# A transformer block on one core: the order of the first loads, and copies of two transposed tiles in pieces

## The chip, the cores and the metric

The kernel runs on one core of a Trainium2 chip. The metric is the time on the device in microseconds (us) of one execution; lower is better. A core has a matrix engine (TensorE, PE in the profile), three engines for elementwise work (VectorE or DVE, ScalarE or ACT, GpSimd or POOL), a queue for transfers and barriers (SyncE or SP) and 16 DMA engines that all queues share. The engines run side by side and wait for each other by semaphores.

## The reference

```python
def _A_ref(x, wqkv, w_phi, wo):          # H = 32 heads of Dh = 20, D = 640
    qkv = (x @ wqkv) ...                  # q, k, v by head
    pq = einsum("bhsd,hdf->bhsf", q, w_phi); pk = einsum("bhsd,hdf->bhsf", k, w_phi)
    phi_q = concatenate([softmax(pq), softmax(-pq)]); phi_k = concatenate([softmax(pk), softmax(-pk)])
    kv = einsum("bhsf,bhsd->bhfd", phi_k, v); z = phi_k summed over s
    o = (phi_q @ kv) / (phi_q . z + 1e-6)
    return o @ wo
def _B_ref(x, w_gate, w_up, w_down):      # F = 1536
    return (gelu(x @ w_gate) * (x @ w_up)) @ w_down

h  = x + _A_ref(layernorm(x), ...)        # x: 1 x 2048 x 640, bfloat16
h2 = h + _B_ref(layernorm(h), ...)
```

A block with linear attention over a feature map and a gated feed-forward part; both read a layer norm of their input.

## The kernel before, in words

The 2048 rows of x are 16 tiles of 128 rows (tile t), in four blocks of four (`x_sb[0]` holds tiles 0 to 3). The 640 columns are five chunks of 128. A tile is normalised, transposed into `LN1T` (chunk by chunk, so that the contraction lies on the partitions), and then multiplied with W_v, with W_k folded with w_phi (`Wk2`), and later with W_q folded with w_phi. After that come the attention's output and the feed-forward part. The queues of all engines hold their instructions in the order in which the code writes them; the order in the head of the kernel is written out by hand.

The change lies in the head, the first 12 us:

- **Transfers.** SP issues x tile 0 (L189), x tile 1 (L190), x tile 2 (L193), W_v chunks 0 and 1 (L194), chunks 2 and 3 (L195), x tile 3 (L196), W_v chunk 4 (L197), x tiles 4 and 5 (L198), and then five transposing loads of W_k into `WkT` (L203). ACT's queue issues w_phi (L191) and then loads the table of ACT's functions (L192). w_phi has one reader, DVE's `BD` (L433), which `fold` needs.
- **TensorE's filler.** `warm` runs matmuls on a constant, with no use for their result, at the start (L230) and after the first transposes (L447).
- **Tiles 0 and 1.** DVE takes the mean off (`ln_0`, `xc_a`), TensorE transposes the five chunks into a PSUM tile (`tr_c`, by `transpose_to`, L164), and ACT copies the whole into `LN1T` (L165). The scale of the norm is applied when v is evicted (`v_ev`, L316).
- **Tile 2 and tile 3.** `ln_st` takes two half statistics (L121) and their aggregate (L125) on DVE, ACT makes the inverse root out of a logarithm and an exponential (L131, L132; `log` says when they are queued), DVE normalises (`ln_ap`, L156), TensorE transposes, and DVE copies (`ln_tp`, L165). `between` queues something between the two half statistics: for tile 3 it is the transposing and copying of tile 2.
- **v.** `v_part(t, chunks)` multiplies the named chunks of tile t with those of W_v, two matmuls of 320 columns a chunk, into one PSUM tile (L312). PSUM has four such buffers here, taken in turn by filler, transposes and accumulators.
- **What comes next.** After v of tile 2 (`v_part(2, ...)`) TensorE transposes tile 3 and folds W_k (L248), and the loop over the tiles begins.

Of the kernel before, what the change touches and what calls it, by code (L numbers as in the profile page):

```python
# [8 lines left out]
BF16 = mybir.dt.bfloat16  # L9
# [8 lines left out]
def kernel(  # L18
# [12 lines left out]
    nc = tc.nc  # L31
    P = 128
    S = 2048
    D = 640
# [5 lines left out]
    NC = D // P  # L40
# [34 lines left out]
    w_v = A_wqkv.rearrange("(c p) n -> p c n", p=P)  # L75
# [4 lines left out]
    psG = ps_cm.enter_context(tc.tile_pool(name="psG0", bufs=4, space=PSUM, reuse_waits="tile"))  # L80
# [16 lines left out]
    ident = const.tile([P, P], BF16, name="ident")  # L97
# [13 lines left out]
    def gtile(name):  # L111
        return psG.tile([P, 2, 512], F32, name=name, tag="G")

    def ln_stats(pool, tiles, tag, act=True, between=None, log=False):

        n = len(tiles)
        mv = small(pool, [P, n, nc.vector.BN_AGGR_DIM], "mv" + tag)
        stats = small(pool, [P, n, 2, nc.vector.BN_STATS_DIM], "stats" + tag)
        for j, xt in enumerate(tiles):
            for i in range(2):  # L120
                nc.vector.bn_stats(stats[:, j, i, :], xt[:, i * HD:(i + 1) * HD])  # L121
                if between and i == j == 0:
                    between()
        for j in range(n):
            nc.vector.bn_aggr(mv[:, j, :], stats[:, j])  # L125
        ve = small(pool, [P, n], "ve" + tag)
        rstd = small(pool, [P, n], "rstd" + tag)
        if log is not False:

            def root():  # L130
                nc.scalar.activation(ve, mv[:, :, 1], ACTF.Ln, bias=eps)  # L131
                nc.scalar.activation(rstd, ve, ACTF.Exp, scale=-0.5)  # L132

            if log is True:
                root()
            else:
                log.append(root)
        else:
            nc.gpsimd.tensor_scalar_add(ve, mv[:, :, 1], EPS)
            nc.gpsimd.tensor_tensor(rstd, ve, nhalf[:, 0:n], op=ALU.pow)  # L140

        mr = small(pool, [P, n], "mr" + tag)
        if act:
            for j in range(n):
                nc.gpsimd.tensor_scalar(mr[:, j:j + 1], mv[:, j, 0:1], rstd[:, j:j + 1], -1.0,
                                        op0=ALU.mult, op1=ALU.mult)
        return [(xt, mv[:, j, 0:1], rstd[:, j:j + 1], mr[:, j:j + 1]) for j, xt in enumerate(tiles)]
# [11 lines left out]
    def transpose_to(dst, src, on_pe, on_dve=False):  # L159

        if on_pe:
            tp = psG.tile([P, 16, P], BF16, name="tp", tag="G")
            for c in range(NC):
                nc.tensor.transpose(tp[:, c, :], src[:, c * P:(c + 1) * P], ident)  # L164
            (nc.vector.tensor_copy if on_dve else nc.scalar.copy)(dst, tp[:, 0:NC, :])  # L165
        else:
            nc.sync.dma_start_transpose(dst, src)
# [4 lines left out]
    LN1T = [LN1F.bitcast(BF16).rearrange("p (b c n) -> p b c n", b=NB, c=NC)[:, b] for b in range(NB)]  # L172
# [3 lines left out]
    Wv = p1.tile([P, NC, D], BF16, name="Wv")  # L176
# [11 lines left out]
    nc.gpsimd.memset(eps, EPS)  # L188
    nc.sync.dma_start(x_sb[0][:, 0:1, :], x_v[:, 0:1, :])  # L189
    nc.sync.dma_start(x_sb[0][:, 1:2, :], x_v[:, 1:2, :])  # L190
    nc.scalar.dma_start(wphi, phi_v.rearrange("(c p) f -> p c f", p=P))  # L191
    nc.scalar.add_instruction(mybir.InstLoadActFuncSet(name=nc.get_next_instruction_name(), act_func_set_id=6))  # L192
    nc.sync.dma_start(x_sb[0][:, 2:3, :], x_v[:, 2:3, :])  # L193
    nc.sync.dma_start(Wv[:, 0:2, :], w_v[:, 0:2, 2 * D:3 * D])  # L194
    nc.sync.dma_start(Wv[:, 2:4, :], w_v[:, 2:4, 2 * D:3 * D])  # L195
    nc.sync.dma_start(x_sb[0][:, 3:4, :], x_v[:, 3:4, :])  # L196
    nc.sync.dma_start(Wv[:, 4:5, :], w_v[:, 4:5, 2 * D:3 * D])  # L197
    nc.sync.dma_start(x_sb[1][:, 0:2, :], x_v[:, 4:6, :])  # L198

    def load_T(WT, i, *ds):  # L200
# [25 lines left out]
    def warm(*cols):  # L226
        for n in cols:
            nc.tensor.matmul(wu[:, 0, 0:n], lhsT=ones[:, 0:P], rhs=ones[:, 0:n], start=True, stop=True)
# [37 lines left out]
    def ln_0(t):  # L266
        xt, mean, rstd, mr = lnp[t] = ln_stats(p1, [x_sb[0][:, t, :]], f"c{t}", False, None, True)[0]
        nc.gpsimd.tensor_scalar(nrstd[t], rstd, -1.0, None, op0=ALU.mult)
        if t == 0:
            nc.gpsimd.tensor_scalar(mr, mean, nrstd[0], None, op0=ALU.mult)  # L270
        xc = fp.tile([P, D], BF16, name="xc", bufs=2)
        nc.vector.tensor_scalar(xc, xt, mean, None, op0=ALU.subtract)
        return xc

    def ln_st(*tiles, act=True, between=None, log=False):
        for t, v in zip(tiles, ln_stats(p1, [x_sb[t // 4][:, t % 4, :] for t in tiles], "1", act, between, log)):
            lnp[t] = v

    def ln_ap(t, on_act=False, on_pe=False):
        ln = (ln_act if on_act else ln_dve)(p1, "1", *lnp[t])  # L280
        if on_pe:
            lnp[t] = ln
        else:
            transpose_to(LN1T[t // 4][:, :, t % 4 * P:(t % 4 + 1) * P], ln, False)

    def ln_tp(t, on_dve=False):
        transpose_to(LN1T[t // 4][:, :, t % 4 * P:(t % 4 + 1) * P], lnp[t], True, on_dve)

    def lnT(t, c):
        b, tl = divmod(t, 4)  # L290
        return LN1T[b][:, c, tl * P:(tl + 1) * P]
# [14 lines left out]
    def v_part(t, *cs):  # L306

        if 0 in cs:
            pv[t] = gtile("pv")
        for c in cs:  # L310
            for u in range(2):
                nc.tensor.matmul(pv[t][:, u, 0:HD], lhsT=lnT(t, c), rhs=Wv[:, c, u * HD:(u + 1) * HD],  # L312
                                 start=(c == 0), stop=(c == NC - 1))

    def v_ev(t):
        nc.scalar.activation(vS[t % NV][:, :, 1:VC].rearrange("p (u h) f -> p u h f", u=2),  # L316
                             pv[t][:, :, 0:HD].rearrange("p u (h f) -> p u h f", f=Dh), ACTF.Copy,
                             scale=lnp[t][2] if t in CT else 1.0)
# [111 lines left out]
    def bd(c0, c1):  # L430

        n = c1 - c0
        nc.vector.tensor_tensor(BD[:, c0:c1], wphi[:, c0:c1, None, :].to_broadcast([P, n, 8, Dh]),  # L433
                                hmask[:, c0:c1, :, None].to_broadcast([P, n, 8, Dh]), ALU.mult)

    def tr_c(t):
        transpose_to(LN1T[0][:, :, t * P:(t + 1) * P], xc[t], True)

    st_act(1, 0)
    xc = [ln_0(0)]  # L440
    xc.append(xc_a(1))
    tr_c(0)
    tr_c(1)
    ln_st(2, act=False, log=True)
    bd(0, NC)
    st_act(1, 1)
    warm(*[P] * 4)  # L447
    v_part(0, 0, 1)
    v_part(1, 0, 1)
    ln_ap(2, on_pe=True)  # L450
    v_part(0, 2, 3)
    root = []
    ln_st(3, act=False, between=lambda: ln_tp(2, True), log=root)
    v_part(0, 4)
    v_ev(0)
    v_part(1, 2, 3)
    root[0]()
    v_part(1, 4)
    v_ev(1)
    v_part(2, *range(NC))  # L460
    d = ident.rearrange("p (r j) -> p r j", r=4)
# [476 lines left out]
```

## Time and profile before

| | us |
|---|---|
| median of 3 runs | 271.55 (271.33 to 272.35) |
| the profiled execution | 272.35 |
| its span in the trace | 270.6 |
| TensorE busy | 266.1 (98% of the span) |
| VectorE busy | 173.9 (64%) |
| ScalarE busy | 138.6 (51%) |
| GpSimd busy | 101.2 (37%) |

The profiled execution is the slowest of the three runs. Its span is the time from the first to the last instruction in the trace; 1.75 us lie around it. Rows of a timeline give start, length, engine, line, operation, and what is written from what; in square brackets stands the idle time of the engine ahead of it and what ended it. Rows that merge several instructions give their number at the end. A busy TensorE is not one at its peak, since the ends of pipelined matmuls are modelled. The granted clock is 1.00 in all of the trace.

### The profile page before, as it was taken

To read this page: it belongs to the slowest core of one execution; us is meant where nothing else is said; L and a number is where in the kernel's file an instruction comes from. 1 tells how busy PE (TensorE), PEld (TensorE's weight loads), DVE (VectorE), ACT (ScalarE), POOL (GpSimd) and SP (SyncE) were. 2 spreads that over 40 slices of the span, in tenths; PEclk is the share of its full clock that TensorE was granted. 3 is DMA by queue.
4 is the path that set the end of the run, shared out by engine and by line. 5 is a ranking of instruction groups with operands and counts; after the bars stand their busy time and mean duration, and the time that the engine had idled before them with its cause. 6 is when DMAs were issued, how large, how long until landed. Compare 5 with 4: busy or idle time off the path is not lost.

```text
span 270.6 us, 7029 instructions
## 1 busy us (share of the span) xinstructions
PE 266.1 (98%) x2857; PEld 172.0 (64%) x2857; DVE 173.9 (64%) x347; ACT 138.6 (51%) x249; POOL 101.2 (37%) x238
## 2 busy tenths in 40 slices
PE   8999999999999999999999999999999999999995
PEld 6777777765455887788755455775555476444574
DVE  5789999996877767876566783568673332333322
ACT  5779997877789675245541356421544300322100
POOL 5448898887002335376211564014661100000000
DMA  6987489213864442432301222203222101000011
GB/s 187 206 199 169 81 210 96 46 37 85 326 201 112 157 101 55 68 78 50 51 27 51 48 50 48 50 3 75 76 46 51 24 24 51 24 0 0 4 48 48
DMA packets 45264, 22.10 MB, mean 82 GB/s; under 512 B 37808, under 2 KB 43184, under 8 KB 45232
## 3 DMA queue, kind: packets, MB, share of 16 engines
q1 hardware_dynamic: 44576, 21.64, 33.5%
q8 instruction: 22, 0.36, 0.6%
q10 hardware_dynamic: 656, 0.03, 0.2%
q14 instruction: 10, 0.08, 0.1%
HBM read 10.18 MB, written 2.62 MB: 47 GB/s over the span
## 4 chain that ended last, share of the span: by engine, by line
PE 96%; DMA 2%; SPq 0%; DVE 0%; issue 0%
PE gu L768 39%; PE pd L790 19%; PE pq L396 8%; PE pk L296 8%; PE po L708 8%; PE pv L296 7%; DMA Wv<-in_A_wqkv_dram 2%; PE kvp L374 2%; PE pv L312 2%; PE ab L619 1%; PE wa L248 1%; PE ab L586 1%; PE tp L164 0%; SPq L193 0%; SPq L190 0%; SPq L189 0%
## 5 line engine op out<-in xcount | busy, mean ns | idle before, releaser
L771 ACT ACTIVATE g<-gu 128x512 bf16<-128x512 f32 (+1 forms) x60 | 30.4, 510 | 74.0 <-PE gu L768 73.2
L774 DVE TENSOR_TENSOR GT<-gu,g 128x512 bf16<-128x512 f32 (+1 forms) x60 | 34.3, 579 | 46.8 <-PE gu L768 38.6
L768 PE MATMUL gu<-LN2T,Wg 128*128 128x512 bf16 (+1 forms) x300 | 61.8, 337 | 0.0
L768 PE MATMUL gu<-LN2T,Wu 128*128 128x512 bf16 (+1 forms) x300 | 61.8, 336 | 0.0
L790 PE MATMUL pd<-Wd,GT 128*128 128x320 bf16 (+4 forms) x396 | 53.9, 295 | 0.0
L790 PEld LDWEIGHTS <-GT 128*128 128x128 bf16 x396 | 37.6, 98 | 14.5 <-DVE GT L774 0.2
L768 PEld LDWEIGHTS <-Wu 128*128 128x128 bf16 x300 | 29.4, 98 | 22.6
L768 PEld LDWEIGHTS <-Wg 128*128 128x128 bf16 x300 | 29.1, 98 | 21.2
L296 PEld LDWEIGHTS <-LN1T 128*128 128x128 bf16 x290 | 28.0, 98 | 10.4
L355 POOL TENSOR_TENSOR E<-E,rs 128x640 bf16<-128x640 bf16 x25 | 31.7, 1295 | 4.4 <-DVE rs L351 2.8
L792 DVE TENSOR_TENSOR y<-pd,x_sb 128x320 bf16<-128x320 f32 (+4 forms) x33 | 15.8, 480 | 24.1 <-PE pd L790 24.1
L708 PE MATMUL po<-Wo,oT 128*128 128x320 bf16 x160 | 24.5, 299 | 0.0
L296 PE MATMUL pk<-Wk,LN1T 128*128 128x320 bf16 x160 | 24.4, 299 | 0.0
L396 PE MATMUL pq<-LN1T,Wq 128*128 128x512 bf16 x100 | 22.9, 379 | 0.0
L347 DVE TENSOR_REDUCE sk<-E 128x64 f32<-128x1280 bf16 x16 | 22.9, 1430 | 0.0
L401 ACT ACTIVATE Eq<-pq 128x1024 bf16<-128x1024 f32 (+1 forms) x26 | 19.9, 831 | 2.8 <-PE pq L396 2.7
L340 ACT ACTIVATE E<-pk 128x640 bf16<-128x640 f32 x28 | 19.1, 769 | 3.0 <-PE pk L296 3.0
L708 PEld LDWEIGHTS <-oT 128*128 128x128 bf16 x160 | 15.6, 98 | 7.3 <-ACT oT L165 0.2
L296 PE MATMUL pv<-Wv,LN1T 128*128 128x320 bf16 x130 | 19.8, 299 | 0.0
L151 ACT ACTIVATE ln<-x_sb,v,rstd 128x640 bf16<-128x640 bf16 x14 | 12.9, 920 | 13.0 <-POOL v L747 12.9
L396 PEld LDWEIGHTS <-Wq 128*128 128x128 bf16 x100 | 9.4, 98 | 10.3
L683 DVE TENSOR_TENSOR tt<-AB,w 128x1280 bf16<-128x1280 f32 x10 | 15.1, 1505 | 0.4 <-POOL w L676 0.3
(120 smaller groups left out, 291.4 us busy)
## 6 DMA issues: line engine op xcount, KB each, us to landing
out_dram<-y SPq DMA_DIRECT2D x15, 160.0 KB, 1.8
x_sb<-in_A_x_dram SPq DMA_DIRECT2D x6, 320.0 KB, 3.3
Wd<-in_B_w_down_dram SPq DMA_DIRECT2D x1, 1440.0 KB, 6.8
Wg<-in_B_w_gate_dram SPq DMA_DIRECT2D x1, 1152.0 KB, 7.3
Wu<-in_B_w_up_dram SPq DMA_DIRECT2D x1, 1152.0 KB, 5.6
Wo<-in_A_wo_dram SPq DMA_DIRECT2D x1, 800.0 KB, 5.0
Wg<-in_B_w_gate_dram SPq DMA_DIRECT2D x1, 768.0 KB
Wu<-in_B_w_up_dram SPq DMA_DIRECT2D x1, 768.0 KB, 9.1
```

The source lines that it names most:

```text
L296: nc.tensor.matmul(ps[:, u, 0:HD], lhsT=lnT(t, c), rhs=W[:, c, u * HD:(u + 1) * HD], start=(c == 0), stop=(c == NC - 1))
L340: nc.scalar.activation(Ek[t][:, s, :].rearrange("p (u f) -> p u f", u=2), pk[:, :, 0:HD], ACTF.Exp, scale=((lnp[t][2], nrstd[t]) if t in C ...
L347: nc.vector.reduce_sum(sk, Ek[t].rearrange("p s (h f) -> p (s h) f", f=Dh), axis=AX.X)
L355: eng.tensor_tensor(e, e, rs[:, s * H:(s + 1) * H, None].to_broadcast([P, H, Dh]), ALU.mult)
L396: nc.tensor.matmul(pqs[j][:, i, :], lhsT=Wq2[:, kc, c * P:(c + 1) * P], rhs=LN1T[b][:, kc, :], start=(kc == 0), stop=(kc == NC - 1))
L401: nc.scalar.activation(Eq[j][:, :, s, :], pqs[j][:, 0:len(QG[j])], ACTF.Exp, scale=(1.0, -1.0)[s])
L708: nc.tensor.matmul(pos[u], lhsT=st[t][:, c, :], rhs=Wo[:, c, u * HD:(u + 1) * HD], start=(c == 0), stop=(c == NC - 1))
L768: nc.tensor.matmul(gu[i][:, 0:n], lhsT=W[:, c, f * P:(f + 1) * P], rhs=LN2T[b][:, c, a0:a1], start=(c == 0), stop=(c == NC - 1))
L771: nc.scalar.activation(g[:, 0:n], gu[0][:, 0:n], ACTF.Gelu_apprx_tanh)
L774: nc.vector.tensor_tensor(st[b, "g", f][:, a0:a1], gu[1][:, 0:n], g[:, 0:n], ALU.mult)
L790: nc.tensor.matmul(pd[:, 0:f1 - f0], lhsT=st[b, "g", f][:, tl * P:(tl + 1) * P], rhs=Wd[:, f, f0:f1], start=(f == 0), stop=(f == NF - 1), ...
L792: nc.vector.tensor_tensor(y[:, f0:f1], pd[:, 0:f1 - f0], x_sb[b][:, tl, f0:f1], ALU.add)
```

## The change

- w_phi is issued after the load of ACT's table instead of before it.
- W_v chunk 0 is loaded ahead of x tile 2; chunks 1 and 2 follow x tile 2, then chunks 3 and 4, then x tile 3. The number of SP's issues is the same.
- The copies of transposed tiles 0 and 1 are no longer two whole copies on ACT. ACT copies chunks 0 and 1 of tile 0; DVE copies its chunks 2 to 4, between the two half statistics of tile 2; ACT copies chunks 0 and 1, and then 2 to 4, of tile 1. The root for tile 2 is queued on ACT behind these.
- The v matmuls of tiles 0 and 1 follow the new pieces: chunk 0 of both, chunks 1 and 2 of both, then chunks 3 and 4 of tile 0, its eviction, the transposes of tile 2, and chunks 3 and 4 of tile 1.

```diff
     nc.sync.dma_start(x_sb[0][:, 1:2, :], x_v[:, 1:2, :])
+    nc.scalar.add_instruction(mybir.InstLoadActFuncSet(name=nc.get_next_instruction_name(), act_func_set_id=6))
     nc.scalar.dma_start(wphi, phi_v.rearrange("(c p) f -> p c f", p=P))
-    nc.scalar.add_instruction(mybir.InstLoadActFuncSet(name=nc.get_next_instruction_name(), act_func_set_id=6))
+    nc.sync.dma_start(Wv[:, 0:1, :], w_v[:, 0:1, 2 * D:3 * D])
     nc.sync.dma_start(x_sb[0][:, 2:3, :], x_v[:, 2:3, :])
-    nc.sync.dma_start(Wv[:, 0:2, :], w_v[:, 0:2, 2 * D:3 * D])
-    nc.sync.dma_start(Wv[:, 2:4, :], w_v[:, 2:4, 2 * D:3 * D])
+    nc.sync.dma_start(Wv[:, 1:3, :], w_v[:, 1:3, 2 * D:3 * D])
+    nc.sync.dma_start(Wv[:, 3:5, :], w_v[:, 3:5, 2 * D:3 * D])
     nc.sync.dma_start(x_sb[0][:, 3:4, :], x_v[:, 3:4, :])
-    nc.sync.dma_start(Wv[:, 4:5, :], w_v[:, 4:5, 2 * D:3 * D])
     nc.sync.dma_start(x_sb[1][:, 0:2, :], x_v[:, 4:6, :])
...
+    tpc = []
+
     def tr_c(t):
-        transpose_to(LN1T[0][:, :, t * P:(t + 1) * P], xc[t], True)
+        tpc.append(psG.tile([P, 16, P], BF16, name="tp", tag="G"))
+        for c in range(NC):
+            nc.tensor.transpose(tpc[t][:, c, :], xc[t][:, c * P:(c + 1) * P], ident)
+
+    def cp_c(t, a, b, on_dve=False):
+        (nc.vector.tensor_copy if on_dve else nc.scalar.copy)(LN1T[0][:, a:b, t * P:(t + 1) * P], tpc[t][:, a:b, :])
...
     tr_c(0)
     tr_c(1)
-    ln_st(2, act=False, log=True)
+    cp_c(0, 0, 2)
+    root = []
+    ln_st(2, act=False, between=lambda: cp_c(0, 2, NC, True), log=root)
+    cp_c(1, 0, 2)
+    cp_c(1, 2, NC)
+    root[0]()
     bd(0, NC)
     st_act(1, 1)
     warm(*[P] * 4)
-    v_part(0, 0, 1)
-    v_part(1, 0, 1)
+    v_part(0, 0)
+    v_part(1, 0)
+    v_part(0, 1, 2)
+    v_part(1, 1, 2)
     ln_ap(2, on_pe=True)
-    v_part(0, 2, 3)
+    v_part(0, 3, 4)
+    v_ev(0)
     root = []
     ln_st(3, act=False, between=lambda: ln_tp(2, True), log=root)
-    v_part(0, 4)
-    v_ev(0)
-    v_part(1, 2, 3)
+    v_part(1, 3, 4)
     root[0]()
-    v_part(1, 4)
     v_ev(1)
     v_part(2, *range(NC))
```

## The prediction

> **What bounds the kernel now.** I read the page first, then the waits of TensorE, then the timelines of the engines over the first 12 us, and last the landing times of the head's transfers.
>
> ```profile
> span 270.6 us, 7029 instructions
> ...
> PE 266.1 (98%) x2857; PEld 172.0 (64%) x2857; DVE 173.9 (64%) x347; ACT 138.6 (51%) x249; POOL 101.2 (37%) x238
> ...
> PE 96%; DMA 2%; SPq 0%; DVE 0%; issue 0%
> ```
>
> TensorE is busy for 98% of the span, and 96% of the chain that ended last is TensorE. Its waits over the whole span are these two:
>
> ```profile
> PE pv L312 <- DMA Wv<-in_A_wqkv_dram: 0.9, 1, 0.9
> PE wu L228 <- PEq L922: 0.8, 1, 0.8
> ```
>
> The second is the start of the program. So there is one stall of 0.9 us to win, and every stall that the change adds behind it moves the end by its length, since TensorE waits nowhere later and has no slack in which to catch up. TensorE's timeline shows where the stall lies:
>
> ```profile
> 4.88 1.25 PE L164 MATMUL tp<-ident,xc 128*128 128x128 bf16 x10
> 5.92 0.63 PE L228 MATMUL wu<-const-bfloat16-1.0 128*128 128x128 bf16 x4
> 7.41 1.79 PE L312 MATMUL pv<-Wv,LN1T 128*128 128x320 bf16 x12 [0.85 <-DMA Wv<-in_A_wqkv_dram]
> 9.03 0.44 PE L164 MATMUL tp<-ident,ln 128*128 128x128 bf16 x5
> 9.31 2.61 PE L312 MATMUL pv<-Wv,LN1T 128*128 128x320 bf16 x18
> 11.76 0.45 PE L164 MATMUL tp<-ident,ln 128*128 128x128 bf16 x5
> 12.04 0.64 PE L248 MATMUL wa<-BD,WkT 128*128 128x140 bf16 x9
> ```
>
> Columns: start, length, what. Filler ends at 5.92 + 0.63 = 6.55 us and the v matmuls start at 7.41. Twelve of them take 9.03 - 7.41 = 1.62 us, 0.135 each. After 9.03 nothing is marked as a wait. I use the start of the transposes of tile 3 (11.76) as the finishing post: the program behind it is the same in both versions, so what that point gains or loses is what the kernel gains or loses.
>
> The landings come from the answers for the issuing lines (first start, then issue to landing):
>
> ```profile
> L193 SPq DMA_DIRECT2D x_sb<-in_A_x_dram x1: 424/424/424, 1.7 to 1.7; - x1
> ...
> DMA to landing us min/median/max: 3.8/3.8/3.8
> ...
> L194 SPq DMA_DIRECT2D Wv<-in_A_wqkv_dram x1: 433/433/433, 2.2 to 2.2; - x1
> ...
> DMA to landing us min/median/max: 5.2/5.2/5.2
> ...
> L195 SPq DMA_DIRECT2D Wv<-in_A_wqkv_dram x1: 469/469/469, 2.7 to 2.7; - x1
> ...
> DMA to landing us min/median/max: 5.5/5.5/5.5
> ...
> L196 SPq DMA_DIRECT2D x_sb<-in_A_x_dram x1: 467/467/467, 3.2 to 3.2; - x1
> ...
> DMA to landing us min/median/max: 5.4/5.4/5.4
> ```
>
> So x tile 2 landed at 1.7 + 3.8 = 5.5, the first two chunks of W_v at 7.4, the next two at 8.2, x tile 3 at 8.6. One slot is 160 KB (a tile of x or a chunk of W_v). From 7.4 to 8.6 a slot took 0.4 us (three slots in 1.2), but from 5.5 to 7.4 two slots took 1.9. At the later rate W_v would have been there at 6.3, before the filler ended. The stall is therefore about one slow stretch of 1.0 us in the transfers.
>
> **Own time and median.** The profiled execution took 272.35 us (span 270.6 and 1.75 around it), the slowest of the three; the median is 271.55, 0.80 lower. That is the size of the stall. My reading, not shown, is that the median run had little of it.
>
> **The change, part by part.**
>
> *W_v chunk 0 into the third slot, x tile 2 into the fourth.* Chunk 0 takes the place of a transfer of its size that landed at 5.5, so it is in time for 6.55: TensorE's wait for W_v goes. But x tile 2 lands one slot later: 5.9 at 0.4 a slot, 6.4 at half of 1.9, 7.0 if the slow stretch falls ahead of it whole (7.4 less one slot). I take 6.4. DVE's row is where that counts:
>
> ```profile
> 5.57 0.89 DVE L121 BATCH_NORM_STATS2 stats<-x_sb 128x6 f32<-128x320 bf16 x2 [0.32 <-DMA x_sb<-in_A_x_dram]
> 6.49 0.21 DVE L125 BATCH_NORM_AGGREGATE mv<-stats 128x2 f32<-128x12 f32 x1
> 6.62 0.94 DVE L433 TENSOR_TENSOR BD<-wphi,hmask 128x800 bf16<-128x800 bf16 x1
> 7.48 0.44 DVE L156 TENSOR_SCALAR ln<-x_sb,mv,rstd 128x640 bf16<-128x640 bf16 x1
> 8.61 0.49 DVE L121 BATCH_NORM_STATS2 stats<-x_sb 128x6 f32<-128x320 bf16 x1 [0.68 <-DMA x_sb<-in_A_x_dram]
> 9.51 0.49 DVE L165 COPY LN1T<-tp 128x640 bf16<-128x640 bf16 x1 [0.41 <-PE tp L164]
> 9.92 0.48 DVE L121 BATCH_NORM_STATS2 stats<-x_sb 128x6 f32<-128x320 bf16 x1
> 10.44 0.21 DVE L125 BATCH_NORM_AGGREGATE mv<-stats 128x2 f32<-128x12 f32 x1
> 11.25 0.45 DVE L156 TENSOR_SCALAR ln<-x_sb,mv,rstd 128x640 bf16<-128x640 bf16 x1 [0.24 <-ACT rstd L132]
> ```
>
> *Copies in pieces.* Three chunks of transposed tile 0 go to DVE, between the two halves of the statistics of tile 2. In the queue order DVE cannot copy before x tile 2 has landed and half a statistic (0.89 / 2 = 0.45) is done. The copy itself lies between 3/5 of the whole one (0.29) and the whole one (0.49); I take 0.35. And TensorE waits for it early: the accumulator of tile 1 gets the PSUM buffer from which tile 0 is copied (four buffers: filler, two transposes, one accumulator), so already the first matmul of tile 1 needs DVE's copy. Behind that matmul the whole in-order stream of TensorE is queued. So after two matmuls for tile 0 at 6.55, TensorE goes on at 6.4 + 0.45 + 0.35 + 0.05 = 7.25. This is the new wait, in the place of the old.
>
> *ACT.*
>
> ```profile
> 0.79 0.46 ACTq L191 DMA_DIRECT2D wphi<-in_A_w_phi_dram  x1
> 1.28 1.28 ACT L192 ACT_TABLE_LOAD   x1 [1.28 <-PEq L922]
> 5.63 1.29 ACT L165 COPY LN1T<-tp 128x640 bf16<-128x640 bf16 x2 [0.37 <-PE tp L164]
> 6.80 0.31 ACT L131 ACTIVATE ve<-mv,eps 128x1 f32<-128x1 f32 x1
> 9.78 0.79 ACT L316 ACTIVATE vS<-pv,rstdc 128x640 bf16<-128x640 f32 x1 [1.63 <-PE pv L312]
> ```
>
> The two whole copies are over at 6.92. The pieces that stay on ACT hold seven chunks of ten and one more start, so they are no later than that, ahead of 7.25: no cost. The logarithm for tile 2 moves with its statistics; the Square queued behind it has the 1.63 us of idle ahead of 9.78 to move into. If that cover went, the eviction of tile 0 and the root for tile 3 would be late with it.
>
> *W_v in one, two, two.* Chunks 1 and 2 fill slots five and six: 7.4 was the end of five slots, so they are there at 7.8. TensorE does two matmuls of tile 1 (7.25 to 7.52), waits to 7.8, does twelve more, and is at the transposes of tile 2 at 9.42. Chunks 3 and 4 are there at 8.6, ahead of the last four of these: nothing. x tile 3 moves one slot, 8.6 to 9.0; its use below is at 9.1, 0.1 of cover.
>
> *w_phi behind the table load.*
>
> ```profile
> wphi<-in_A_w_phi_dram ACTq DMA_DIRECT2D x1, 25.0 KB, 2.8
> ```
>
> It was issued at 0.79 (row above; the table load follows at 1.28), so it was there at 3.6; behind the load it is between unchanged and 1.28 later, 4.9. Its reader on DVE stands at 8.0 by the sum below: no cost. It leaves the way of x tiles 0 and 1, by at most its own share of the transfers, which can bring forward only work that waits for x tile 2 anyhow. SP still has six issues here before the W_k transposes, so those keep their times.
>
> **The sum.** DVE: x tile 2 at 6.4, half statistic to 6.85, copy to 7.20, other half to 7.65. From the end of the statistics to the normalised tile the rows give 7.92 - 6.46 = 1.46: 9.11. TensorE arrives at 9.42 and so starts tile 2's transposes 0.39 after the 9.03 of before. From there the chain is as it was: copy (9.51), second half of the statistics of tile 3 (9.92), aggregate, root, normalise (11.25), all 0.39 later, and the transposes of tile 3 at 12.15 instead of 11.76. TensorE itself would be there at 11.78 (copy done at 10.39, ten matmuls), so DVE's chain ends last. That is +0.39 against the profiled execution: 272.74.
>
> Against a run without the slow stretch the same steps give: before, v at 6.55, transposes of tile 2 at 8.17, of tile 3 at 10.9 (TensorE the last). After: x tile 2 at 5.9, copy done 6.70, fourteen matmuls from 6.82 to 8.71, normalised tile 2 at 8.61, so tile 2's transposes at 8.71 and tile 3's 0.54 later than before. Both pairings say +0.4 to +0.5. I take +0.4 on the median: 271.95.
>
> **The rivals.**
>
> *The stall goes and nothing takes its place.* If the slow stretch belongs to the order of the transfers and not to chance, it is in the profiled before and not in the after: x tile 2 at 5.9, tile 3's transposes at 8.71 + 2.73 = 11.44, 0.32 earlier than 11.76, so 271.2; with everything of the stall, 0.85, 270.7. For it: 0.4 us per slot in three of five slots. Against it: the median already lies low by the size of the stall.
>
> *x tile 2 lands last.* At 7.0 the DVE copy ends at 7.80 and the statistics at 8.25, tile 2 is normalised at 9.71, and tile 3's transposes come 0.7 late; with x tile 3 late behind it, 1.0: 272.55. Above 1.4 late it is slower by my bound. It decides from a landing of 7.0 on.
>
> *The clock of TensorE stays low: slower.* Rows above: ten transposes from 4.88 to 5.92 are 104 ns each, five from 9.03 to 9.31 are 56 ns each. So TensorE ran at half rate until 5.92 at least and at full rate from 7.41 on (the matmuls of 320 columns there are 0.135 apart). The change lets it idle from two matmuls after 6.55 until 7.25, where the filler alone stood before. If the idle time keeps the rate down, the twenty matmuls of tiles 0 and 1 and ten of tile 2 cost about 0.27 instead of 0.135 (320 columns at twice the time): 30 x 0.135 = 4.0 us, 275.5. It decides if the first matmul of tile 1 still runs at half rate. Against it: as long an idle time, 0.85, did not hold the rate down in the profiled run. [...]
>
> *The change does nothing at all*, the copies being hidden and slots equal: within the forecast's range, 271.55.
>
> **How the numbers follow.** Forecast, with the no-effect case in it: 0.56, 271.95. Stall gone: 0.27, 271.2. x tile 2 last: 0.10, 272.55. Low clock: 0.07, 275.5. The range reaches from just under the second (271.0) to above the third (272.9), leaving out the low clock and the tails. The bound of 0.5% is 1.36 us, about what a measurement of this kernel can tell from no change. Faster than 270.19 needs more than the whole stall: 0.03. Slower than 272.91: the low clock and 0.04 of the third case, 0.11. Within: 0.86.
>
> **What would show it.** Right: TensorE's wait for W_v is gone, a wait for DVE's copy of tile 0 stands behind the second v matmul at 7.0 to 7.5, the transposes of tile 3 wait for DVE and start after those of before. Wrong: x tile 2 read by DVE before 5.9, no wait of TensorE for DVE ahead of tile 1, tile 3's transposes before 11.4, or v matmuls more than 0.2 us apart without a marked wait.

## The result, and the profile after

| | before | after |
|---|---|---|
| median (range) | 271.56 us (271.33 to 272.35), 6 runs | 273.39 us (273.13 to 273.64), 6 runs |
| ratio | 1 | 1.0064 (95% interval 1.005 to 1.0078) |

The change makes the kernel 1.83 us slower. The profiled execution of after took 273.47 us. Its page:

```profile
span 271.7 us, 7031 instructions
...
PE 266.2 (98%) x2857; PEld 171.4 (63%) x2857; DVE 174.3 (64%) x348; ACT 139.1 (51%) x250; POOL 101.3 (37%) x238
...
PE 94%; DVE 2%; DMA 1%; SPq 0%; issue 0%; ACT 0%
```

TensorE is as busy as before (266.1), but the chain that ended last holds 2% of DVE (0% in before) and less of the transfers. TensorE's waits over the whole span say where:

```profile
PE pd L802 <- DVE GT L786: 1.3, 1, 1.3
PE wu L228 <- PEq L934: 0.8, 1, 0.8
PE pv L312 <- DVE LN1T L444: 0.3, 1, 0.3
PE tp L164 <- DVE ln L156: 0.2, 1, 0.2
```

The wait for W_v is gone. The third and fourth rows are the head, and small. The first is the largest and lies far from any line that the change touches: L802 is the down projection of the feed-forward part. TensorE's timeline of the head (start, length, what, idle time before it):

```profile
4.80 0.92 PE L441 MATMUL tp<-ident,xc 128*128 128x128 bf16 x10
5.56 0.39 PE L228 MATMUL wu<-const-bfloat16-1.0 128*128 128x128 bf16 x4
5.82 0.45 PE L312 MATMUL pv<-Wv,LN1T 128*128 128x320 bf16 x2
6.59 2.06 PE L312 MATMUL pv<-Wv,LN1T 128*128 128x320 bf16 x14 [0.32 <-DVE LN1T L444]
8.48 0.44 PE L164 MATMUL tp<-ident,ln 128*128 128x128 bf16 x5
8.76 2.28 PE L312 MATMUL pv<-Wv,LN1T 128*128 128x320 bf16 x14
11.21 0.45 PE L164 MATMUL tp<-ident,ln 128*128 128x128 bf16 x5 [0.16 <-DVE ln L156]
```

The v matmuls begin at 5.82 instead of 7.41, and tile 3's transposes at 11.21 instead of 11.76. So at the finishing post of the prediction this execution was 0.55 us ahead of the profiled before, and it still ended 1.1 us later (271.7 against 270.6). The loss is behind that point. TensorE of after, and then of before, where the gate and up projections (`gu`) of one part hand over to the down projection (`pd`):

```profile
102.16 0.71 PE L780 MATMUL gu<-LN2T,Wg 128*128 128x256 bf16 x5
102.70 0.71 PE L780 MATMUL gu<-LN2T,Wu 128*128 128x256 bf16 x5
104.75 2.62 PE L802 MATMUL pd<-Wd,GT 128*128 128x326 bf16 x18 [1.33 <-DVE GT L786]
```

```profile
102.60 0.71 PE L768 MATMUL gu<-LN2T,Wg 128*128 128x256 bf16 x5
103.15 0.71 PE L768 MATMUL gu<-LN2T,Wu 128*128 128x256 bf16 x5
103.69 2.62 PE L790 MATMUL pd<-Wd,GT 128*128 128x326 bf16 x18
```

From the start of the last `gu` matmuls to the first `pd` it is 0.54 us in before (103.69 - 103.15) and 2.05 in after (104.75 - 102.70): 1.51 us lost in one place. DVE at that time, after first, then before:

```profile
102.02 1.49 DVE L695 TENSOR_TENSOR tt<-AB,w 128x1280 bf16<-128x1280 f32 x1
103.54 0.49 DVE L699 TENSOR_TENSOR o<-tt 128x640 bf16<-128x640 bf16 x1
103.95 0.75 DVE L786 TENSOR_TENSOR GT<-gu,g 128x256 bf16<-128x256 f32 x2
```

```profile
101.17 0.36 DVE L774 TENSOR_TENSOR GT<-gu,g 128x256 bf16<-128x256 f32 x1
...
102.46 1.49 DVE L683 TENSOR_TENSOR tt<-AB,w 128x1280 bf16<-128x1280 f32 x1
103.98 0.49 DVE L687 TENSOR_TENSOR o<-tt 128x640 bf16<-128x640 bf16 x1
104.39 0.75 DVE L774 TENSOR_TENSOR GT<-gu,g 128x256 bf16<-128x256 f32 x2
```

DVE's queue is the same in both: the last two products of gate and up stand behind attention work and end at 104.70 in after and at 105.14 in before. In before `pd` starts at 103.69, before either of them has begun, so the first `pd` matmuls do not need their data. In after `pd` starts at 104.75, 0.05 behind the end of the last. What `pd` waits for in after is therefore not the product but the PSUM buffer that the product is read from. (This is read from the order of the rows here; the experiments below show it.)

**The theory.** The tiles that TensorE writes lie in PSUM (`space=PSUM` in the code), first in the pool `psG`, with four buffers of 2 x 512 float32 numbers per partition. A stretch of 512 is called a bank here, so these are buffers of two banks, numbered 0 to 7. At the handover `split()` closes `psG` and opens `psB` with eight buffers of one bank, and the first `pd` takes bank 0. Followed through the two programs, the last tiles take these buffers (named by their first bank):

```
before:  ... gu:0  po:4  gu:6  gu:2 | pd:0
after:   ... gu:2  po:4  gu:6  gu:0 | pd:0
```

In before bank 0 was last used by the third-last `gu`, whose product was done at 101.53 (101.17 + 0.36); in after by the very last. Buffers 0 and 2 have changed places from tile 3's transposes to the handover: in before the accumulator of v of tile 2 was in 4, tile 3's transposes in 0 and the first fold in 2; in after the last two are exchanged. The reason is one edit: v of tile 0 is finished and evicted (`v_part(0, 3, 4)`, `v_ev(0)`) ahead of tile 2's transposes, so in the order of the code its buffer is given back ahead of theirs (in time the copy of tile 2 ended first in both traces, at 10.00 in before and 9.46 in after, beside 10.57 and 9.49 for the eviction). Both programs ask for the same tiles in the same order, so what decides is the order in which the code gives buffers back; "taken in turn", as the words on the kernel before have it, is not exact. "The turn" stands below for which buffer each tile gets. The rivals were that the loss comes from the loads and copies of the head in some other way (data of the head that reach `pd` late), or from chance.

`pd` waits for the buffer as a whole, not for the bank that it writes. A `gu` tile holds the gate in its first bank (`gu[:, 0]`), which ACT reads, and the up projection in its second (`gu[:, 1]`), which DVE reads for the product. The first `pd` writes only the first. ACT had read the gate from it by 103.90 (row of after):

```profile
103.51 0.39 ACT L783 ACTIVATE g<-gu 128x256 bf16<-128x256 f32 x1
```

For 0.85 us more, until 104.75, `pd` waits for the reader of the other bank. The pools are opened with `reuse_waits="tile"`; that this is what joins the two banks is a reading of the code, and no run lets `pd` wait for its own bank alone.

### The profile page after: what moved, and what is told of

It is laid out like the page before. It is cut to its first block, busy times and chain, and to the rows that moved or that the text cites. A ratio compares the mean times of both kernels' runs of the same rounds, so it can differ in the third digit from the quotient of the medians.

```text
span 271.7 us, 7031 instructions
## 1 busy us (share of the span) xinstructions
PE 266.2 (98%) x2857; PEld 171.4 (63%) x2857; DVE 174.3 (64%) x348; ACT 139.1 (51%) x250; POOL 101.3 (37%) x238
## 4 chain that ended last, share of the span: by engine, by line
PE 94%; DVE 2%; DMA 1%; SPq 0%; issue 0%; ACT 0%
PE gu L780 38%; PE pd L802 19%; PE pq L396 8%; PE pk L296 8%; PE po L720 8%; PE pv L296 7%; PE kvp L374 2%; PE ab L631 1%; DMA x_sb<-in_A_x_dram 1%; PE wa L248 1%; PE ab L598 1%; PE pv L312 1%; DVE tt L695 1%; PE tp L164 0%; DVE stats L121 0%
## 5 line engine op out<-in xcount | busy, mean ns | idle before, releaser
L802 PE MATMUL pd<-Wd,GT 128*128 128x320 bf16 (+4 forms) x396 | 53.9, 295 | 1.3 <-DVE GT L786 1.3
L802 PEld LDWEIGHTS <-GT 128*128 128x128 bf16 x396 | 37.7, 98 | 15.9 <-issue 1.5
```

The costliest lines, as they stand in the source:

```text
L802: nc.tensor.matmul(pd[:, 0:f1 - f0], lhsT=st[b, "g", f][:, tl * P:(tl + 1) * P], rhs=Wd[:, f, f0:f1], start=(f == 0), stop=(f == NF - 1), ...
```

## The experiments

**1. After, with the buffers turned back.** One more tile, with one matmul of 32 columns, takes a buffer ahead of tile 3's transposes.

```diff
+    sk = gtile("sk")
+    nc.tensor.matmul(sk[:, 0, 0:32], lhsT=ones[:, 0:P], rhs=ones[:, 0:32], start=True, stop=True)
     ln_tp(3, True)
```

> The changed kernel with one more PSUM buffer taken and given back ahead of the transposes of tile 3 (a matmul of 32 columns on a constant, some 0.05 us), so that all later tiles sit in the buffers in which they sit in the kernel before. Theory A (buffers): TensorE's wait of 1.3 us at 103.4 us is there because the first accumulator of the down projection gets the buffer of the last gate-and-up pair; with the old turn the wait goes, and the time is 273.4 - 1.6 = 271.8 us. Theory B (the elementwise engines are late there for another reason, an effect of the new order in the head): the wait stays, 273.4 us.

Measured: 272.24 us beside 271.81, ratio 1.0017 (1.0008 to 1.0025). The wait of `pd` is gone from the trace; TensorE's rows of this kernel:

```profile
11.15 0.18 PE L482 MATMUL sk<-const-bfloat16-1.0 128*128 128x32 bf16 x1
11.47 0.45 PE L164 MATMUL tp<-ident,ln 128*128 128x128 bf16 x5
...
102.91 0.71 PE L782 MATMUL gu<-LN2T,Wu 128*128 128x256 bf16 x5
103.46 2.62 PE L804 MATMUL pd<-Wd,GT 128*128 128x326 bf16 x18
```

`pd` follows 0.55 us behind the start of the last `gu` matmuls again. The added matmul stands in its row with 0.18 us, where 0.05 was expected. With one matmul more, the loss against before falls from 1.83 to 0.43 us. What stays is of the size that the prediction gave the head (+0.4).

**2. Before, with the same two lines.** It shifts the turn of before, and the first `pd` now gets the buffer of the second-last `gu`.

> The kernel before with the same added matmul and nothing else. It turns the buffers so that the first accumulator of the down projection gets the buffer of the last gate-and-up pair but one. Theory A: TensorE waits until VectorE has read that pair, which in the profile before ended near 104.8 us against a start of 103.69: about 1.1 us slower, 272.65 us. Theory B: no part of the change is in it, 271.6 us.

Measured: 273.14 us beside 271.81, ratio 1.005 (1.0036 to 1.0065).

```profile
103.47 0.71 PE L770 MATMUL gu<-LN2T,Wu 128*128 128x256 bf16 x5
105.18 0.99 PE L792 MATMUL pd<-Wd,GT 128*128 128x326 bf16 x6 [1.00 <-DVE GT L776]
```

The same two lines that take 1.4 us off the loss of after put 1.33 on before. The wait is 1.00 and not 1.33: with the second-last product's buffer it ends earlier by one product, half of the 0.75 that two take.

**3. Before, with only the eviction written early.** No load and no copy of the change is in it.

```diff
-    root = []
-    ln_st(3, act=False, between=lambda: ln_tp(2, True), log=root)
     v_part(0, 4)
     v_ev(0)
+    root = []
+    ln_st(3, act=False, between=lambda: ln_tp(2, True), log=root)
```

> The kernel before with v_part(0, 4) and v_ev(0) written ahead of the statistics of tile 3, as the change has them, so that the buffers stand as in the changed kernel from the transposes of tile 3 on: the first accumulator of the down projection gets the buffer of the last gate-and-up pair. No load and no copy is changed; two matmuls change places with the transposes of tile 2. Theory A (buffers): VectorE ended that last pair near 105.1 us in the profile before, against a start of 103.69: 1.4 to 1.5 us slower than before, ratio 1.005 or more, and more than with the buffer of the last pair but one. Theory B: within 0.2 us of before.

Measured: 273.43 us beside 271.72, ratio 1.0065 (1.0053 to 1.0077).

```profile
11.19 0.45 PE L164 MATMUL tp<-ident,ln 128*128 128x128 bf16 x5
...
102.71 0.71 PE L768 MATMUL gu<-LN2T,Wu 128*128 128x256 bf16 x5
104.75 1.54 PE L790 MATMUL pd<-Wd,GT 128*128 128x326 bf16 x10 [1.34 <-DVE GT L774]
```

Two statements in another order give the whole loss of the change, 1.0065 beside 1.0064, with the same wait at the same place. That settles the cause of the 1.5 us.

**4. Before, with only the new order of SP's loads** (W_v chunk 0 ahead of x tile 2, and W_v in the new pieces; w_phi as in before).

> The kernel before with the new order and pieces of the loads alone (W_v chunk 0 ahead of x tile 2, then 1 and 2, 3 and 4, x tile 3); copies, matmul order and buffers as before. If tile 2 through VectorE ends last, a slot of 0.4 us later for tiles 2 and 3 costs 0.2 to 0.4 us: 272.0 to 272.2 us beside a before of 271.8. If the early W_v chunk is worth more, it is faster than before by 0.3 us or more.

Measured: 271.71 us beside 271.72, ratio 1.0003 (0.9995 to 1.0012). Neither branch of the expectation came true: neither the loss nor a gain comes from these loads.

**5. Before again, one execution.**

> The kernel before, for a second trace of it. If the stall of 0.85 us on W_v in the profiled run was chance (one slow transfer), the v matmuls start by 6.7 us here, the transposes of tile 3 near 11.0 instead of 11.76, and the time is near 271.6 us. If it belongs to the order of the transfers, W_v lands near 7.4 again.

Measured: 271.44 us, span 269.7. TensorE's rows:

```profile
6.52 1.79 PE L312 MATMUL pv<-Wv,LN1T 128*128 128x320 bf16 x12 [0.41 <-DMA Wv<-in_A_wqkv_dram]
8.15 0.44 PE L164 MATMUL tp<-ident,ln 128*128 128x128 bf16 x5
8.43 2.61 PE L312 MATMUL pv<-Wv,LN1T 128*128 128x320 bf16 x18
10.87 0.45 PE L164 MATMUL tp<-ident,ln 128*128 128x128 bf16 x5
```

In an execution close to the median v starts at 6.52, 0.89 earlier than in the profile that the prediction was made from. With the same loads it started at 6.69 in experiment 2, 6.51 in experiment 3 and 6.29 in the last run below, so the 7.41 was chance, as the prediction read it (it had 6.55, 8.17 and 10.9 for such a run). That 6.52 is so near to 6.55 is partly luck: the prediction's run had no wait for W_v and a filler that ended at 6.55; here the filler ended at 6.10, and 0.41 us of waiting for W_v followed. Against this execution the head of after is 0.34 us late, not 0.55 early.

**6. What is left in the head.** Seven variants look for the 0.1 to 0.2% that stay with the buffers turned back. The first experiment with the old order of SP's loads:

> e1_after_turn with the loads in the order and pieces of before (w_phi behind the table load stays); the copies in pieces and the new order of the v matmuls stay. If the chain from x tile 2 through VectorE ends last in the head, tile 2 lands earlier by a slot and the time is 0.2 to 0.4 us under e1_after_turn, 271.5 us. If the earlier W_v chunk is what gave the head its 0.55 us, the wait for W_v is back and the time is some 0.5 us above it, 272.3 us.

Measured: 272.45 us, ratio 1.0031 (1.0018 to 1.0044); tile 3's transposes at 11.39. With the old loads it is not faster. The time is near the 272.3 of the second branch, but the wait for W_v that this branch names is not in the trace. The first experiment with tile 0's chunks 2 to 4 copied on ACT (`cp_c(0, 2, NC)`) instead of on DVE:

> e1_after_turn with chunks 2 to 4 of tile 0 copied by ScalarE instead of VectorE, right behind chunks 0 and 1. If VectorE's copy, queued behind the statistics of tile 2, costs what the prediction said (TensorE waits 0.32 us for it, and VectorE's chain is 0.34 longer), the time is about 0.3 us under e1_after_turn, 271.5 us. If both are hidden, the same as e1_after_turn.

Measured: 271.99 us, ratio 1.0017 (1.0006 to 1.0029); tile 3's transposes at 11.12. The ratio is that of the first experiment, so no gain of the engine of the copy is shown; the interval, 0.6 us wide, does not exclude the expected 0.3. This one with x tile 2 loaded ahead of W_v chunk 0, meant to beat both kernels:

> A version meant to beat both: the buffers turned back, all copies of tiles 0 and 1 on ScalarE in pieces, W_v in one, two, two, but x tile 2 ahead of W_v chunk 0 as in before. Tile 2 is at VectorE as early as before and chunk 0 lands near 5.8: the v matmuls start at about 6.1 instead of 6.5 to 6.7, and if the rest follows the time is 0.2 to 0.4 us under before, 271.5 us beside 271.8. If VectorE's chain to tile 3 ends last all the same, the same as before.

Measured: 272.37 us, ratio 1.0036 (1.0023 to 1.0049). A miss: in its profile, of the fastest of six executions, v starts at 6.06, as expected, but tile 3's transposes at 11.20, later than the 10.87 of before.

Next came tile 2's transposes ahead of the eviction in after, which turns the buffers back with no added matmul:

```diff
+    root = []
+    ln_st(3, act=False, between=lambda: ln_tp(2, True), log=root)
     v_part(0, 3, 4)
     v_ev(0)
-    root = []
-    ln_st(3, act=False, between=lambda: ln_tp(2, True), log=root)
     v_part(1, 3, 4)
```

> The changed kernel with one edit: tile 2's transposes are written ahead of the eviction of W_v's product for tile 0 and of its last chunks, as in the kernel before. Nothing is added. Two things follow from it: tile 2's transposes and the accumulators take their buffers in the order of the kernel before, so that the first matmul of the down projection gets the third-last gate-and-up buffer again; and 12 instead of 14 to 16 matmuls of v stand ahead of tile 2's transposes. Theory of the buffers: the wait for DVE's last gate-and-up product (1.3 us) and the rest of the 1.6 us at 103 us are gone, without the extra matmul of the first experiment: at most 272.2. Theory of the head (the later place of tile 2's transposes is what is left): also up to 0.3 off the first experiment's 272.24, so 271.6 to 271.9, a ratio of 0.999 to 1.001; if what is left of the head comes from x tile 2's later transfer and not from the matmuls ahead, 272.1 to 272.4 as in the first experiment. If the loss at 103 us had nothing to do with the buffers' turn: 273.4.

Measured: 272.08 us beside 271.54, ratio 1.0017 (1.0006 to 1.0028). TensorE's rows:

```profile
5.93 1.98 PE L312 MATMUL pv<-Wv,LN1T 128*128 128x320 bf16 x12
8.26 0.45 PE L164 MATMUL tp<-ident,ln 128*128 128x128 bf16 x5 [0.35 <-DVE ln L156]
8.55 2.61 PE L312 MATMUL pv<-Wv,LN1T 128*128 128x320 bf16 x18
11.07 0.45 PE L164 MATMUL tp<-ident,ln 128*128 128x128 bf16 x5
...
102.55 0.71 PE L780 MATMUL gu<-LN2T,Wu 128*128 128x256 bf16 x5
103.09 2.62 PE L802 MATMUL pd<-Wd,GT 128*128 128x326 bf16 x18
```

The buffers' part holds once more: exchanging two statements of after removes the wait of `pd`. The other half of the expectation fell. With 12 instead of 16 matmuls ahead, tile 2's transposes wait 0.35 us for DVE's normalised tile, and the ratio is that of the first experiment. So the number of matmuls ahead is not shown to be what remains. The same kernel with all copies on ACT and x tile 2 first:

> The kernel of the run before (tile 2's transposes written early), with all copies of tiles 0 and 1 on ScalarE in pieces, and x tile 2 loaded ahead of the first row chunk of W_v. It is the candidate to beat both kernels: the buffers turn as before, v's first matmul can start some 0.3 to 0.5 us earlier than in the kernel before (6.1 against 6.52), and 12 matmuls stand ahead of tile 2's transposes. Theory that the head's length is what is gained: tile 2's transposes near 7.9 (8.15 in the second profile of the kernel before), tile 3's at 10.8 or earlier (10.87), 271.3 to 271.5 beside 271.7, a ratio of 0.998 to 0.9995. Theory that DVE's chain from tile 2 to tile 3 sets the head whatever v does: 271.6 to 271.9, no difference from the kernel before. If the first experiment's extra matmul rather than the buffers had been what helped: 273.4.

Measured: 272.03 us, ratio 1.0012 (1.0 to 1.0025), so it does not beat before. In its profiled execution TensorE waited 0.57 us for a piece of W_v that came late. Last, the two halves of what is left, each by itself: the kernel with tile 2's transposes early, its copies whole on ACT,

> The changed kernel with tile 2's transposes written early, as in an earlier run (272.08, ratio 1.0017), and besides both transposed tiles copied whole on ScalarE, as in the kernel before; what is left of the change is the order of the loads and of v's matmuls. It is to find the 0.1 to 0.2% that stay when the loss at 103 us is gone. If they come from the copies in pieces: no difference from the kernel before, a ratio of 0.9995 to 1.0008, 271.5 to 271.7. If they come from the order of v's matmuls with the order of the loads: 1.0012 to 1.0025 as in that run, 271.9 to 272.2.

and before with nothing but the copies in pieces:

> The kernel before with the copies of the transposed tiles 0 and 1 in pieces as the only edit (tile 0: two chunks on ScalarE, three on VectorE between the halves of tile 2's statistics; tile 1: two and three on ScalarE); loads, v's matmuls and buffers as before. If the copies in pieces are what is left of the loss: a ratio of 1.001 to 1.0025, 271.8 to 272.2, with tile 3's transposes 0.2 to 0.5 us later than in the kernel before (10.87). If they are not: 0.9995 to 1.0008.

Measured: 271.91 us, ratio 1.0008 (0.9995 to 1.0021), and 271.94 us, ratio 1.0001 (0.999 to 1.0012), both beside 271.77. Neither half can be told from no change. The interval of the copies alone ends below the 1.0017 of the first experiment; that of the other half does not. The 0.1 to 0.2% that they have together is not traced to one of them; it stays open.

**The kernels at the finishing post.** One profiled execution each; the last column is the span less the third column, that is, the time behind the start of tile 3's transposes.

| kernel | wait of `pd` | tile 3's transposes | span | behind them |
|---|---|---|---|---|
| before, first profile | none | 11.76 | 270.6 | 258.8 |
| before, again (5) | none | 10.87 | 269.7 | 258.8 |
| after, turned back (1) | none | 11.47 | 270.4 | 258.9 |
| after, tile 2 early (6) | none | 11.07 | 270.0 | 258.9 |
| new loads only (4) | none | 11.59 | 270.7 | 259.1 |
| after | 1.3 | 11.21 | 271.7 | 260.5 |
| eviction early (3) | 1.3 | 11.19 | 271.7 | 260.5 |
| before, turned (2) | 1.0 | 11.07 | 272.1 | 261.0 |

Where the turn is that of before, the time behind the post is 258.8 to 259.1 us, wherever the post lies. The other six kernels of experiment 6, which the table leaves out, have that turn too, 258.8 to 259.1 and no wait of `pd`. With the exchanged buffers it is 260.5. (The 261.0 is from the slowest execution of its kernel, 0.7 us above the median. It holds two waits for transposed tiles, 0.4 us in all, which the others lack, and, with the shorter wait of `pd`, some 0.4 us more that is not explained.)

## Why the prediction was wrong, point by point

**The step that failed** is the sentence on the finishing post: "the program behind it is the same in both versions, so what that point gains or loses is what the kernel gains or loses." The instructions behind it are the same and in the same order on every engine, but their PSUM buffers are not. Two of the four are exchanged from the head to the handover, 92 us later, and there it decides what `pd` waits for. The prediction did follow the buffers' turn, to the first matmul of tile 1, and stopped there. Against the second profile of before, after loses 0.34 us in the head, 0.12 between there and the last `gu` matmuls (91.49 against 91.37 us), 1.51 at the handover and 0.03 behind it: 2.0 in the span.

**The price was in the trace of before.** DVE's last product ended at 105.14 and `pd` had started at 103.69. If the buffer of the last product had been `pd`'s, it would have cost 1.45 us. The wait and the gap measured 1.33 and 1.51.

**No slack on TensorE** was right, and it is why the handover cost its full length: from the first `pd` to the end it is 166.9 us in both (271.7 - 104.75 and 269.7 - 102.78).

**W_v's stall by chance** was right for the slow stretch: TensorE's wait for the first two chunks ended at 7.41 in the first profile of before and at 6.52 in the second. It was not right for all of the wait, of which 0.41 us was left there. The rival in which the stall goes and nothing takes its place, 271.2, was wrong: something does take its place (below), and most of what goes from the profile was not in the median.

**x tile 2 a slot later, and the copy on DVE.** Rows of after, first the landing of W_v chunk 0 and x tile 2, then DVE:

```profile
L193 SPq DMA_DIRECT2D Wv<-in_A_wqkv_dram x1: 437/437/437, 1.7 to 1.7; - x1
...
DMA to landing us min/median/max: 3.6/3.6/3.6
...
L194 SPq DMA_DIRECT2D x_sb<-in_A_x_dram x1: 432/432/432, 2.2 to 2.2; - x1
...
DMA to landing us min/median/max: 3.6/3.6/3.6
```

```profile
5.78 0.49 DVE L121 BATCH_NORM_STATS2 stats<-x_sb 128x6 f32<-128x320 bf16 x1 [0.57 <-DMA x_sb<-in_A_x_dram]
6.20 0.34 DVE L444 COPY LN1T<-tp 128x384 bf16<-128x384 bf16 x1
```

x tile 2 was there at 5.8; the prediction had 5.9 for a run without the slow stretch and took 6.4 for the sum. DVE read it from 5.78, and from 5.57 and 5.69 in the two profiles of before, so the slot cost 0.1 to 0.2 us, not 0.4 or more. The copy took 0.34 (0.35). TensorE's new wait for it stands behind the second v matmul, as predicted, and ended at 6.59 (6.82 for x tile 2 at 5.9, 7.25 for 6.4). Tile 2's transposes came at 8.48 (8.71), tile 3's 0.34 later than in before again (0.54). So this chain is there in the trace, somewhat shorter than predicted. Its size on the median, +0.4, is near the +0.43 of experiment 1 and the +0.54 of the reordered after, but that these come from this chain is not shown: with the copy on ACT the ratio of experiment 1 stayed. The rival with x tile 2 last did not come up.

**The signs.** Of the signs that the prediction named for being right, the wait for W_v was gone, the wait for DVE's copy stood where it should (but ended at 6.59, not at 7.0 to 7.5), and tile 3's transposes waited for DVE; they started after those of the second profile of before, not of the first. Two of its signs of being wrong came up: DVE read x tile 2 before 5.9 (5.78), and tile 3's transposes started before 11.4 (11.21). Both say that the head was faster than the sum, and neither points at the handover.

**The loads.** W_v's new order and pieces alone moved the median by nothing (experiment 4). w_phi was issued at 0.82 instead of 0.79 (last section), the lower end of the predicted 0 to 1.28, and landed after 2.7 us, at 3.5 (3.6 in before). Its reader on DVE started at 7.10, so its move cost nothing there.

**The low clock** did not come: the 14 v matmuls from 6.59 to 8.48 are 0.135 us apart, although TensorE had idled 0.32 just before.

**The chances.** Slower by over 0.5% had 0.11, most of it for the low clock. It came true by a mechanism that was not among the rivals.

Both programs rotate their groups of matmuls through the PSUM buffers; the runs show that at the seam between the two pools it is the phase of the rotation that counts, 1.0 to 1.3 us of waiting in the kernels with the wrong one and none in the others.

## What to carry to other kernels

When a change moves the point at which a buffer of a rotating pool is taken or given back, compare which buffer every later tile gets, above all the first tile behind a change of pools, before calling the rest of the program the same. Count the readers of the whole old buffer, not only those of the bank that is written again (here `pd` started 0.85 us after the reader of its own bank was done). The price of a bad turn can be estimated from the trace of the kernel before: it is the time from the start of the first new writer to the end of each late reader of the old tiles (1.45 us here, beside 1.33 to 1.51 measured). And where the queues are unchanged and a new wait stands between two engines, see whether the waiting instruction needs the other's data or only its buffer; in the second case one exchange of two statements, or one idle tile, can remove it.

## What the runs showed of the hardware

The landing of the head's transfers differed between two executions of the same program by more than the 0.4 us that the change was predicted to cost: TensorE's wait for the first two chunks of W_v ended at 7.41 us in one execution of before and at 6.52 in the other. TensorE waited for W_v 0.85 us in the first and 0.41 in the second, 0.59 in that of the new loads alone, 0.57 in the last candidate and not at all in after. In after, the transfer that is queued on ACT behind the table load did not wait for the load's end:

```profile
0.79 1.28 ACT L191 ACT_TABLE_LOAD   x1 [0.79 <-PEq L934]
0.82 0.45 ACTq L192 DMA_DIRECT2D wphi<-in_A_w_phi_dram  x1
```

The transfer of w_phi was issued at 0.82 while the load ran until 2.07, so this edit moved it by 0.03 us from the 0.79 of before.
